# One mask of the first unit moved to ScalarE and GpSimd, and a new order of the early loads, in a fused gated-attention and feed-forward kernel

## The chip, the cores and the metric

The kernel runs on one core of one Trainium2 chip. The metric is the device time of one execution in microseconds (us); the median of three executions before the change is 182.77 us. The profiled execution of the kernel before spans 181.1 us from its first to its last instruction.

## What is computed

For 4 batches and 8 heads, a recurrence runs over 768 tokens with a state of 48x48 per head; the output, laid out as 3072 tokens by 384, goes through a two-layer feed-forward net with an exact gelu between. Cut to what matters:

```
f = 1 / (1 + exp(-f_logit))
for t in range(768):
    state = f[t][:, None] * state + outer(k[t], v[t])     # per batch and head, 48 x 48
    y[t]  = q[t] @ state
h   = x @ w_in                      # x: 3072 x 384 (all y), w_in: 384 x 2048
out = gelu_exact(h) @ w_out         # w_out: 2048 x 384
```

Inputs and the output are float32 in HBM.

## The kernel before, in words

**Tiling.** Tokens are cut into 24 chunks of 128; two chunks make a *unit* (12 of them, numbered u = 0 to 11). For a unit the recurrence is done in chunk form: decays from `f_logit` (Exp and Ln on ScalarE, cumulative sums on TensorE, then two more Exp), scaled q and k (`sc`, line 576), their transposes (`T`, line 611), scores inside the chunk (`A`, line 784), a triangular mask on them (`mask_scores`, line 621; normally one VectorE product per 128x512 tile, line 631, four for a unit), products with v (`YI`, line 826), the carried state (`S`, lines 806, 655, 657, 662; `YX`, line 705), and a transpose of the result (`XT`, line 691) that gives the feed-forward's input tile `xT`. Units 0 to 4 use a paired layout, in which a partition holds two neighbouring tokens; later units use a natural one.

**Feed-forward.** For each unit `ffn_group` makes 8 steps `F1` (line 875, six matmuls of 128x256 each, into one of four PSUM banks), one Gelu after each (line 885, ScalarE), and then `F2` (line 896), four steps of four matmuls for each of the two chunks, and stores of 128x384. `w_in` lies in three tiles: `win0` holds the columns 0 to 1023 (four of the eight F1 steps), `win1` 1024 to 1535 (two steps), `win2` 1536 to 2047 (two steps). `w_out` lies in four tiles `wout0` to `wout3`, one for each F2 step of a chunk. The profile and the lists of instructions count the tiles of one kernel through: there `win` 70, 71, 72 are `win0`, `win1`, `win2`, and `sc_99`, `sc_100` are the third unit's.

**Order of the work.** No engine's order is written out by hand. Each operation is given to a planner (`Plan`, line 85) with an engine, a duration, dependencies, buffers and a priority; `run` (line 116) places them one after another, by earliest start and then priority, and the instructions are issued in that order. Each engine then runs its list strictly in order. The priorities get a small random term, whose seeds are the list `SEEDS`, one for each unit. So a change of seeds reorders instructions on all engines without adding any.

**Loads.** The list `LOADS` gives the order of the transfers: `f2` is the logits of unit 2, `k2`, `q2`, `v2` its k, q and v, `i0` to `i2` the tiles `win0` to `win2`, `o0` to `o3` the tiles of `w_out`, `u4` all four inputs of unit 4 (`i3` names nothing and is passed over). Inputs of units are issued by SyncE and run on the DMA queue that the profile calls q1; weights are issued by GpSimd, which also casts them to bfloat16, and run on q0. The two queues are kept from overtaking one another by *gates* (`load`, line 382): where the queue changes from one entry to the next, the new transfer waits until an earlier one of the other queue has landed:

```
gate = None
if i and order[i - 1][0] != eng:
    back = 4 if eng == "pool" else 2
    for j in range(i - back, -1, -1):
        if order[j][0] != eng:
            gate = order[j][1]
            break
```

So a load on GpSimd looks four entries back and then on to the next one of SyncE's, and a load on SyncE two entries back. An entry whose predecessor is on its own queue gets no gate.

**Table sets.** Exp and Ln are in one table set of ScalarE and Gelu in another; at each change from one to the other a table load is issued (line 953).

**Junk matmuls.** In the first 30 us, where the plan leaves TensorE idle, matmuls on a tile `junk` are put in (line 947); they compute nothing.

Of the kernel before, what the change touches and what calls it, by code (L numbers as in the profile page):

```python
# [24 lines left out]

SPREAD, SEED = (1.0, 97)

SEEDS = [1643, 41, 3215, 1275, 2533, 2502, 823, 887, 1264, 763, 2447, 3095]

NUDGE = {}  # L30
XA = 0.0
# [53 lines left out]
class Plan:  # L85
# [30 lines left out]
    def run(self):  # L116
        free = dict.fromkeys(list(LAT), 0.7)
        free["DMA"] = 1.8
        rng = random.Random(SEED)
        own = [random.Random(x) for x in SEEDS]  # L120
        for o in self.ops:
            if o.prio > -5:
                k = min(max(int(o.prio % 1000) // 20, 0), len(SEEDS) - 1)
                o.prio += rng.uniform(-SPREAD, SPREAD)
                if SEEDS[k]:
                    w = (0.5, 1.0, 3.0, 8.0)[SEEDS[k] % 4]
                    o.prio += own[k].uniform(-w, w)
# [105 lines left out]
G1D = [2, 3, 4]  # L233
YJ = [2, 3, 4]
ROWS = [16, 17, 18, 19]
AMX = []
WARM = 30.0
LOADS = ['f0', 'k0', 'v0', 'q0', 'f1', 'v1', 'k1', 'q1', 'i0', 'k2', 'f2', 'v2', 'q2', 'i1', 'i2', 'i3', 'o0', 'o1', 'o3', 'o2', 'f3', 'k3', 'q3', 'u4', 'v3']
LOADS += [f"u{n}" for n in range(12) if f"u{n}" not in LOADS and f"c{2 * n}" not in LOADS and f"f{n}" not in LOADS]


@with_exitstack
def kernel(
# [185 lines left out]
    wo_src = moe_w_out.rearrange("(r p j) m -> r p j m", r=4, j=4)  # L429
    for what in LOADS:  # L430
        m = int(what[1:])
# [189 lines left out]
    def mask_scores(aps, ams, key, nm, rd, pr, mk, mkey):  # L621
        for hh in range(2):
            pl = key[1:] + (hh,) in GAM
            if key[1:] + (hh,) in AMX:
                P.add("ACT", 0.50, lambda hh=hh: nc.scalar.copy(ams[hh].t().rearrange("p h t -> p (h t)"), aps[hh].t()),
# [361 lines left out]
```

## Time and profile before

| what | value |
|---|---|
| median of 3 executions | 182.77 us (182.22 to 183.18) |
| span of the profiled execution | 181.1 us |
| TensorE busy | 171.7 us (95%), 10.4 us of it junk |
| ScalarE busy | 125.2 us (69%), 15 table loads of 1283 ns at line 953 |
| VectorE busy | 96.3 us (53%) |
| GpSimd busy | 53.6 us (30%) |
| first F1 matmul | 20.67 us |

TensorE is the engine with the most work. Its busy time must be read with care: junk is counted in it, and matmuls overlap, so that a busy TensorE need not be at its peak. The questions to ask of this profile are when TensorE begins work that counts, and what it waits for after that.

### The profile page before, as it was taken

To read this page: it belongs to the slowest core of one execution; us is meant where nothing else is said; L and a number is where in the kernel's file an instruction comes from. 1 tells how busy PE (TensorE), PEld (TensorE's weight loads), DVE (VectorE), ACT (ScalarE), POOL (GpSimd) and SP (SyncE) were. 2 spreads that over 40 slices of the span, in tenths; PEclk is the share of its full clock that TensorE was granted. 3 is DMA by queue.
4 is the path that set the end of the run, shared out by engine and by line. 5 is a ranking of instruction groups with operands and counts; after the bars stand their busy time and mean duration, and the time that the engine had idled before them with its cause. 6 is when DMAs were issued, how large, how long until landed. Compare 5 with 4: busy or idle time off the path is not lost.

```text
span 181.1 us, 4916 instructions
## 1 busy us (share of the span) xinstructions
PE 171.7 (95%) x1990; PEld 132.3 (73%) x1990; DVE 96.3 (53%) x194; ACT 125.2 (69%) x212; POOL 53.6 (30%) x116
## 2 busy tenths in 40 slices
PE   7788889999999999988999999999999999999993
PEld 2356669966787688785779689976697986886972
DVE  5289750058898564244896692527691625362110
ACT  2775198963899189999967759777585578560720
POOL 7657870003043641140176113112435110300000
PEclk9999999999999999999999999999999999999999
DMA  6999999949997898999999999999999872814102
GB/s 148 261 261 226 268 170 203 200 115 267 278 266 142 186 197 170 249 227 171 216 179 213 215 175 207 195 187 189 185 245 181 181 162 47 166 37 91 43 0 87
DMA packets 106998, 32.61 MB, mean 180 GB/s; under 512 B 102113, under 2 KB 106081, under 8 KB 106977
## 3 DMA queue, kind: packets, MB, share of 16 engines
q1 hardware_dynamic: 105056, 29.07, 79.7%
q0 software_dynamic: 1776, 3.15, 9.8%
q8 instruction: 15, 0.25, 0.6%
q10 hardware_dynamic: 144, 0.10, 0.2%
q14 instruction: 7, 0.05, 0.1%
HBM read 25.17 MB, written 4.72 MB: 165 GB/s over the span
## 4 chain that ended last, share of the span: by engine, by line
PE 64%; ACT 15%; DMA 15%; SPq 3%; issue 1%; DVE 0%; DVEq 0%
PE ps L875 26%; PE ps L896 25%; ACT gT L885 7%; DMA fl<-in_f_logit_dram 7%; DMA win<-in_moe_w_in_dram 5%; ACT L953 4%; SPq L449 3%; DMA kq<-sc 2%; PE ps L722 2%; PE ps L758 2%; PE ps L917 1%; ACT gt L549 1%; PE ps L521 1%; PE ps L699 1%; PE ps L745 1%
## 5 line engine op out<-in xcount | busy, mean ns | idle before, releaser
L885 ACT ACTIVATE gT<-ps 128x512 bf16<-128x512 f32 x96 | 57.5, 671 | 24.6 <-PE ps L875 23.0
L875 PE MATMUL ps<-xT,win 128*128 128x256 bf16 x576 | 68.7, 273 | 1.3 <-ACT gT L885 0.9
L896 PE MATMUL ps<-wout,gT 128*128 128x384 bf16 x368 | 66.0, 326 | 0.0
L875 PEld LDWEIGHTS <-win 128*128 128x128 bf16 x576 | 61.6, 114 | 3.9 <-issue 1.2
L896 PEld LDWEIGHTS <-gT 128*128 128x128 bf16 x368 | 34.2, 98 | 19.5
L583 POOL CAST vb<-vt 128x384 bf16<-128x384 f32 x22 | 12.6, 584 | 52.5 <-DMA vt<-in_v_dram 52.4
L631 DVE TENSOR_TENSOR am<-ps,mask 128x512 bf16<-128x512 f32 x28 | 17.6, 684 | 15.1 <-PE ps L722 15.1
L901 DVE COPY osb<-ps 128x384 f32<-128x384 f32 x20 | 11.1, 556 | 25.9 <-PE ps L896 18.2
L657 POOL TENSOR_TENSOR tn<-rr,gl 128x384 f32<-128x384 f32 x16 | 14.0, 872 | 35.2 <-DVE rr L655 34.6
L576 DVE TENSOR_TENSOR sc<-qt,gt 128x384 bf16<-128x384 f32 x23 | 14.0, 616 | 13.7 <-ACT gt L549 13.7
L576 DVE TENSOR_TENSOR sc<-kt,rg 128x384 bf16<-128x384 f32 x23 | 13.5, 597 | 11.3 <-ACT rg L543 11.3
L953 ACT ACT_TABLE_LOAD x15 | 19.2, 1283 | 0.3
L662 POOL CAST sb<-tn 48x192 bf16<-48x192 f32 x40 | 14.8, 371 | 11.6 <-DVE tn L651 6.6
L494 ACT ACTIVATE fl<-fl 128x768 f32<-128x768 f32 x12 | 10.1, 842 | 10.5 <-DMA fl<-in_f_logit_dram 10.5
L675 DVE CAST yb<-ps 128x384 bf16<-128x384 f32 x22 | 11.9, 555 | 7.4 <-PE ps L758 3.7
L631 DVE TENSOR_TENSOR am<-ps,maskp 128x512 bf16<-128x512 f32 x20 | 12.5, 684 | 2.2 <-PE ps L784 1.4
L543 ACT ACTIVATE rg<-ps 128x384 f32<-128x384 f32 x21 | 10.3, 503 | 4.4 <-PE ps L523 2.8
L549 ACT ACTIVATE gt<-ps 128x384 f32<-128x384 f32 x21 | 10.2, 503 | 3.9 <-PE ps L523 3.3
L947 PE MATMUL ps<-junk 128*128 128x512 bf16 (+3 forms) x36 | 10.4, 423 | 2.1 <-POOL junk L939 1.3
L655 DVE TENSOR_TENSOR rr<-ps,tn 128x384 f32<-128x384 f32 x16 | 8.9, 553 | 3.5 <-POOL tn L657 1.8
L497 ACT ACTIVATE lf<-fl 128x768 bf16<-128x768 f32 x12 | 10.1, 843 | 0.4
L947 PEld LDWEIGHTS <-junk 128*128 128x128 bf16 x36 | 3.6, 111 | 6.2 <-issue 3.5
(74 smaller groups left out, 130.4 us busy)
## 6 DMA issues: line engine op xcount, KB each, us to landing
out_dram<-osb SPq DMA_DIRECT2D x19, 192.0 KB, 3.1
fl<-in_f_logit_dram SPq DMA_DIRECT2D x14, 192.0 KB, 3.8
kt<-in_k_dram SPq DMA_DIRECT2D x14, 192.0 KB, 3.8
qt<-in_q_dram SPq DMA_DIRECT2D x14, 192.0 KB, 3.7
vt<-in_v_dram SPq DMA_DIRECT2D x14, 192.0 KB, 3.9
fl<-in_f_logit_dram SPq DMA_DIRECT2D x5, 384.0 KB, 6.2
kt<-in_k_dram SPq DMA_DIRECT2D x5, 384.0 KB, 6.2
vt<-in_v_dram SPq DMA_DIRECT2D x5, 384.0 KB, 5.7
```

Of the source, the lines that this page charges most:

```text
L549: P.add("ACT", 0.40, lambda g=gps[j], gtv=gtv: nc.scalar.activation(gtv(), g.t()[:, 0:HD].rearrange("q (p h d) -> q p h d", h=2, d=D), AF. ...
L576: P.add("POOL" if pl else "DVE", 0.80 if pl else 0.475, lambda a=a, y=y, j=j, w=w, pl=pl, b=(gtv if w else rg): (nc.gpsimd if pl else nc.v ...
L583: P.add("ACT" if hv else "POOL", 0.40 if hv else 0.47, lambda y=y, j=j, hv=hv: (nc.scalar.copy if hv else nc.gpsimd.tensor_copy)(y["vb"].t ...
L631: P.add("POOL" if pl else "DVE", 1.15 if pl else 0.61, lambda hh=hh, pl=pl: (nc.gpsimd if pl else nc.vector).tensor_tensor(ams[hh].t(), ap ...
L657: P.add("POOL", 0.83, lambda: nc.gpsimd.tensor_tensor(tn.t(), rr.t(), glb(), ALU.mult), rd=[("rr", n), ("gl", n)], wr=[("tn", n)], bufs=[r ...
L662: P.add("POOL", 0.36, lambda hh=hh: nc.gpsimd.tensor_copy(sb.t()[64 * hh:64 * hh + D, :, D * hh:D * hh + D], tn.t()[64 * hh:64 * hh + D, : ...
L675: P.add("ACT" if help_ else "DVE", 0.40 if help_ else 0.475, lambda: copier(help_)(yb.t()[:, i, :], yp.t()[:, 0:HD]), rd=[("yp", n)], wr=[ ...
L875: nc.tensor.matmul(hps.t()[:, i * tok:(i + 1) * tok].rearrange("a (s t) -> a s t", s=s), col(fo)[:, kk, :], xT.t()[:, :, kk, :], start=(kk ...
L885: nc.scalar.activation(to, fr, AF.Gelu)
L896: nc.tensor.matmul(op.t()[:, 0:d_model], gT.t()[:, fo, s_ * C:(s_ + 1) * C], wout[fo // 4][:, fo % 4, :], start=(fo == 0), stop=(fo == FO ...
L947: nc.tensor.matmul(o.opens.t()[:, 0:w], junk[:, 0:C], junk[:, 0:w], start=True, stop=True, skip_group_check=True)
L953: nc.scalar.preload_act_table_set({"exp": "natural_log_exp_and_others", "gelu": "gelu_and_others"}[o.table])
```

## The change

Three edits, and their consequences in the order of the instructions:

```diff
-SEEDS = [1643, 41, 3215, 1275, 2533, 2502, 823, 887, 1264, 763, 2447, 3095]
+SEEDS = [410, 2974, 3123, 787, 3638, 3000, 447, 988, 2575, 1888, 1815, 299]
...
-AMX = []
+AMX = [(0, 0, 1)]
...
-LOADS = ['f0', 'k0', 'v0', 'q0', 'f1', 'v1', 'k1', 'q1', 'i0', 'k2', 'f2', 'v2', 'q2', 'i1', 'i2', 'i3', 'o0', 'o1', 'o3', 'o2', 'f3', 'k3', 'q3', 'u4', 'v3']
+LOADS = ['f0', 'k0', 'v0', 'q0', 'f1', 'v1', 'k1', 'q1', 'f2', 'i2', 'i0', 'k2', 'v2', 'q2', 'i3', 'o0', 'o1', 'i1', 'o3', 'o2', 'f3', 'k3', 'q3', 'u4', 'v3']
```

`AMX` takes one of unit 0's four mask products off VectorE: ScalarE copies the scores from PSUM to SBUF (line 625), and GpSimd multiplies them there with the mask in place (line 627). `LOADS` brings the third unit's logits `f2` ahead of the weights, so that its decays can be computed before ScalarE goes over to Gelu, and brings `win2` ahead of `win0`, so that two of the eight F1 steps can start on a smaller tile; `win1` goes behind two tiles of `w_out`. `SEEDS` gives a new draw of the order.

In the compiled order of the instructions this reads as follows. The third unit's Exp, Ln and its other decay operations (lines 494 to 570) stand before the first table load for Gelu; before the change only its Exp and Ln did. The first F1 steps are two on `win2`, between the two halves of unit 1's score matmuls. The transposes of the third unit's scaled k and q (line 611) stand among the first unit's F1 steps; before, they stood behind all sixteen F1 steps of units 0 and 1. ScalarE has 21 table loads at line 953, before 15. The gates come out anew:

| transfer | waits for, before | waits for, after |
|---|---|---|
| `win0` (i0) | f1 landed | nothing (follows i2 on its queue) |
| `win2` (i2) | nothing (follows i1) | v1 landed |
| `k2` | nothing | `win2` landed |
| `f2` | nothing | nothing |
| `win1` (i1) | k2 landed | nothing (follows o1) |
| `wout0` (o0) | nothing (follows i2) | f2 landed |
| `f3` | `wout3` (o3) landed | `wout3` (o3) landed |

## The prediction

> **What bounds the kernel now.** I read the windows first, then the chain that ended last, then TensorE's timeline and the DMA queues.
>
> ```profile
> 25.00:30.00 5.00, 4.21 (x42) 3.54 (x40) 1.04 (x3) 4.25 (x7) 1.49 (x3) 1.00 1.14 182
> 30.00:35.00 5.00, 5.00 (x49) 5.00 (x47) 0.00 (x0) 5.00 (x10) 0.00 (x0) 1.00 1.08 212
> 35.00:40.00 5.00, 5.00 (x39) 3.29 (x38) 1.88 (x4) 4.33 (x9) 0.00 (x0) 1.00 0.44 94
> ```
>
> The columns are TensorE, weight loads, VectorE, ScalarE, GpSimd (busy us and instructions), clock, DMA share, GB/s. From 30 us TensorE is full; its waits after that are 0.4 us at 55, 0.5 us at 79 and 0.4 us at 84. So the time is the moment from which TensorE does nothing but real work, plus the work left, plus 3 us from the last matmul to the end of the store. A change can win only ahead of about 27 us; a stall that it makes later comes back whole. The chain says what the start waits for:
>
> ```profile
> 10.84 9.78 DMA win<-in_moe_w_in_dram
> 20.67 2.16 PE ps L875 x18
> ```
>
> `win0` is issued at 10.84 and lands at 20.6, and the first F1 follows at once. Then, on TensorE:
>
> ```profile
> 26.38 1.13 PE L947 MATMUL ps<-junk 128*128 128x512 bf16 x5 [0.79 <-ACT gT L885]
> 27.35 8.02 PE L875 MATMUL ps<-xT,win 128*128 128x256 bf16 x72
> 35.21 4.06 PE L896 MATMUL ps<-wout,gT 128*128 128x384 bf16 x24
> 39.11 0.61 PE L611 MATMUL ps<-ident,sc 128*128 128x128 bf16 x8
> ```
>
> From 25.4 to 27.4 TensorE waits for Gelu (2 us, more than half of it junk); then 12 F1 steps without a break, 24 matmuls of F2, and only at 39.1 the third unit's transposes. So k2 and q2 are not wanted before 38 us. The last view is the DMA queues, from 16 to 18 us and from 20 to 22 us:
>
> ```profile
> q0 software_dynamic: 168, 0.34, 90.9%
> q1 hardware_dynamic: 167, 0.06, 19.0%
> ```
> ```profile
> q1 hardware_dynamic: 1470, 0.55, 123.0%
> q0 software_dynamic: 2, 0.00, 0.6%
> ```
>
> (Packets, MB, share of 16 engines.) While `win0` is under way, both queues get the same number of packets. But one of q0 is 2 KB and one of q1 384 B, so q1 moves 0.06 MB in 2 us; alone it moves 0.55. The issues show it too: k2, issued just ahead of `win0`, takes 10.7 us to land, k1 6.2.
>
> ```profile
> kt<-in_k_dram SPq DMA_DIRECT2D x1, 384.0 KB, 10.7
> ```
>
> **What the Trainium skill says.** "DMA: Bandwidth & Descriptors", section "Queues, rings and completion order": each DMA engine goes round robin over its queues, packet by packet. The trace agrees (168 to 167). The same page, "Latency and other measured facts", has two of the 16 engines usually slower; no view here names an engine, but q0 still has 2 packets after 20 us, when an average engine should be done at 19.1 (below). "TensorE: Matmul & The Clock Gate", "What's actually happening": after about 3.4 us idle the array runs at half rate, until busy for about as long. The trace shows the cold start alone: the first 12 junk matmuls take 4.59 us (383 ns each), four later ones 0.92 us (230 each). "ScalarE: Activation LUTs", "What ACT_TABLE_LOAD costs", gives 1283 ns and a drain of 1380; the trace has the 1283, and only 0.3 us idle before all 15, so I take no drain.
>
> **The change, part by part.**
>
> *The mask.* VectorE loses one product of 684 ns. ScalarE gains a 128x512 copy from PSUM, between the 384-column copies (486 ns) and the Gelu of 512 (671): 0.6 us. GpSimd gains a product, not shown in this form: between its 384-column cast scaled by 512/384 (584 to 780 ns) and its 384-column float32 product scaled so (872 to 1163); I take 1.1. Behind the copy wait unit 1's decays, of which one v cast now comes later; behind the product unit 1's scaled k and q. YI of unit 0, at 15.09 before, moves by +0.2. Unit 1's scores move from 18.7 to about 19.5. Both lie ahead of the weights' landing: 0.
>
> *f2 early.* It takes k2's place at 10.32 on SyncE and follows q1 (landed 15.0). 1024 packets at 1376 in 2 us are 1.5 us: landed 16.5, for 22.5 before. ScalarE does unit 2's decays from about 18.6 to 23.2, loads the Gelu table until 24.5, and the 2 us wait at 25.4 goes.
>
> *win2, win0.* GpSimd issues `win2` behind a state product at about 12.4 (v1 lands at 5.87+6.2=12.1) and `win0` at once after. `win1`, of the same size, took 7.3 us from issue: `win2` lands at 19.7. `win0` follows on the queue: 24 packets an engine, with the pair time (one packet of each queue) 2x16/167=0.19 us, less 0.023 (32/1376) while q1 is empty: from 18.5 to 22.7 on an average engine, landing about 24.5. So the two F1 steps on `win2` run at about 20, those on `win0` from 24.8. Were that all: at 27.35 before, four F1 (2.6 us) and XT (0.5) were done; at 24.8 after, two F1 and no XT. Gain 27.35-24.8-1.3-0.5=0.75 us.
>
> *The new gates.* This is the step that decides. k2 waits on SyncE for `win2`'s landing, and v2 and q2 queue behind it: first packets at about 19.7+1.1=20.8 (the first load of all: issued 0.74, packets from about 1.9). `wout0`, gated by f2 alone, is issued at about 18.4, with `wout1` and `win1` right behind. So when k2 begins, q0 holds, for an average engine, 10 packets of `win0`, 8+8 of `wout` (128 of 3 KB each) and 24 of `win1` (1 KB): 50. k2 has 64 an engine and gets one for one. Times of one: `wout` 0.215+0.023 (149 packets in 32 to 34 us, 2x16/149), 1 KB 0.113+0.023 (24 to 26 us: 263 of q0 and 95 of q1 in 2x16). Sum 10x0.19+16x0.24+24x0.136=9.0, and 14x0.023=0.3: k2's last packet at 30.1, landed 31.1. `win0` began at about 14.5 (126 packets by 16 us, at 84 a us), so an average engine needed 4.6 us, the last one 5.6 (packets after 20 us): 1.2 times; over 9 us that is 1.8 more, 32.9. I take 32.5. q0 is then empty, so v2 lands at 34.0 and q2 at 35.5.
>
> Who waits: VectorE holds the third unit's scaled k (`sc_99`) in its strict list, TensorE its transposes behind only two F1 steps on `win0` and the XT. TensorE reaches them at 24.8+1.3+0.5=26.6 and stands until 32.5+0.65=33.2, although eight of the twelve F1 steps queued behind have their weights. After 6.6 us idle it starts cold: transposes 0.4, F1 1.3, transposes 0.4, F1 1.3: 36.6, warm by then; S (v2 at 34.0 plus two GpSimd casts, 35.3) 36.9; F1 37.5; transposes of q (35.5+0.6) 37.8; F1 38.4; VectorE's state sum and last scaled q after S, 38.0; transposes 38.6. From there it is full. Done then: 8 of the 16 F1, all 16 transposes, S. Before, at 38.6: 16 F1 and 3.4 us of F2, no transposes. Lag: 8x0.655+3.4-0.9-0.25=7.5 us. TensorE is saturated after that, so nothing gives it back: **182.8+7.5=190.3**.
>
> *wout3, wout2, f3.* `wout3` is issued behind the casts of v2 and a state product, at about 38.5, and lands about 43; f3, gated by it, about 47, for 41.9 before. ScalarE comes to it at about 48, F2 to `wout2` at about 48 too: 0, narrowly.
>
> *Seeds and table loads.* Six more loads are 6x1.283=7.7 us of ScalarE, which is 69% busy (73% then). They cost only where four PSUM banks of F1 are full and wait for Gelu: 0 to 4 us. I take 0, as F2 and attention stand between. The rest of the draw moves the same matmuls about: 0.
>
> **The rivals.**
>
> (A) Starved loads, as above: 190.3; with an average engine's k2 and no cold clock 188, with the slow engine's and a late f3 194. For it: the equal packet counts, the gates in the compiled order. Against: no window shows q1 beside 3 KB packets.
>
> (B) q1 gets its share, k2 lands by 25 and q2 by 28: nothing stalls, the gain of 0.75 us stays: **182.0**, some 1 us less if the new draw also takes away the later waits of 1.3 us, some 1 more if `win1` (behind 4 us of `wout`) is late. For it: the fast q1 of 20 to 22 us, if `wout` were issued late. Against: 168 to 167.
>
> (C) k2 is not the bound, but ScalarE with its 21 table loads is, in half of the six added: 182.0+3x1.28=**185.8**. For it: ScalarE 16.9 of 20 us from 80 to 100. Against: TensorE waited for Gelu 0.9 us in all after 27 us.
>
> **How the numbers follow.** A 0.74, B 0.14 (0.10 of it faster by over 0.5%, 0.04 within), C 0.12. Faster 0.10, same 0.04, slower 0.86. The likeliest is 190.3. The range takes in A with both ends of its costs and most of C, up to 195 where a late f3 and some table loads come on top; down to 184, below which lies B.
>
> **What would show it.** TensorE idle from about 26 to 33 us ahead of line 611, released by VectorE's `sc` at line 576, itself released by the DMA of `kt`; k2's time to landing over 11 us; equal packet counts of q0 and q1 from 21 to 30 us; unit 2's decays ahead of the first Gelu; first F1 on `win0` near 24.8. I am wrong if k2 lands before 27 us, or if TensorE meets line 611 without a wait.

## The result and the profile after

The changed kernel takes 188.19 us (median of 4 executions, 186.92 to 189.44) against 182.50 of the kernel before: a ratio of 1.030, 95% interval 1.023 to 1.038. It is slower by 5.5 us by this ratio (the two medians lie 5.7 us apart), where 7.5 were forecast. The profiled execution spans 185.2 us, 181.1 before.

The windows of the changed kernel, with the columns as before:

```profile
20.00:25.00 5.00, 5.00 (x61) 2.90 (x60) 3.30 (x7) 2.25 (x5) 2.19 (x5) 0.73 1.10 211
25.00:30.00 5.00, 4.03 (x72) 2.97 (x70) 2.22 (x4) 4.97 (x9) 0.89 (x3) 1.00 1.16 243
30.00:35.00 5.00, 3.80 (x44) 3.51 (x45) 3.32 (x8) 2.30 (x4) 1.54 (x3) 1.00 0.39 83
35.00:40.00 5.00, 5.00 (x74) 4.45 (x72) 3.51 (x6) 3.71 (x6) 2.13 (x5) 1.00 0.67 107
```

TensorE is full from 35 us on, not from 30 as before; and from 20 to 25 us, where its busy time looks full, it was granted 0.73 of its clock. The chain that ended last, in this stretch:

```profile
11.49 0.83 POOL tn L657
...
12.39 7.02 DMA win<-in_moe_w_in_dram
...
19.43 11.13 DMA kt<-in_k_dram
...
30.58 0.57 DVE sc L576
...
31.20 0.40 PE ps L611 x4
31.59 0.66 PE ps L875 x6
```

Before, the chain went from `win0` straight to F1. Now it goes from GpSimd's state product to `win2`, from its landing over the new gate to k2, from k2 to VectorE's scaled k, and from there to the transposes. TensorE's timeline shows the meeting:

```profile
27.19 0.85 PE L875 MATMUL ps<-xT,win 128*128 128x256 bf16 x6
27.88 0.33 PE L691 MATMUL ps<-ident,yb 128*128 128x128 bf16 x3
28.05 0.82 PE L875 MATMUL ps<-xT,win 128*128 128x256 bf16 x6
28.70 0.33 PE L691 MATMUL ps<-ident,yb 128*128 128x128 bf16 x3
31.20 0.40 PE L611 MATMUL ps<-ident,sc 128*128 128x128 bf16 x4 [2.17 <-DVE sc L576]
31.43 0.82 PE L875 MATMUL ps<-xT,win 128*128 128x256 bf16 x6
```

Two F1 steps on `win0` and the XT stand ahead of line 611; then come 2.17 us of nothing, although eight F1 steps queued behind have their weights. The list of TensorE's waits in this kernel:

```profile
PE ps L611 <- DVE sc L576: 3.8, 4, 2.2
```

(us in all, times, longest.) No wait for Gelu is in that list, with 21 table loads. The queues from 22 to 24 us and from 24 to 26 us:

```profile
q0 software_dynamic: 147, 0.40, 100.8%
q1 hardware_dynamic: 67, 0.03, 6.9%
```
```profile
q0 software_dynamic: 179, 0.33, 87.9%
q1 hardware_dynamic: 180, 0.07, 19.1%
```

k2 moves 0.03 MB and then 0.07 MB in 2 us each, beside `wout` and `win1`. In the first of the two windows its packets begin only at about 22.9 us; from 23 to 24 us there are 74 of q0 and 64 of q1. k2 takes 11.1 us to land, v2 12.1 and q2 12.7, counted from issue.

### The profile page after: what moved, and what is told of

Its sections match the earlier page's. It is cut to its first block, busy times and chain, and to the rows that moved or that the text cites. A ratio compares the mean times of both kernels' runs of the same rounds, so it can differ in the third digit from the quotient of the medians.

```text
span 185.2 us, 4914 instructions
## 1 busy us (share of the span) xinstructions
PE 174.2 (94%) x1989; PEld 132.5 (72%) x1989; DVE 97.4 (53%) x193; ACT 133.5 (72%) x219; POOL 54.1 (29%) x117
## 4 chain that ended last, share of the span: by engine, by line
PE 67%; DMA 15%; ACT 10%; DVE 4%; SPq 1%; issue 1%; POOL 1%; DVEq 0%; ACTq 0%
PE ps L875 27%; PE ps L896 27%; DMA kt<-in_k_dram 6%; ACT gT L885 5%; DMA win<-in_moe_w_in_dram 4%; DMA qt<-in_q_dram 3%; DMA kq<-sc 2%; PE ps L722 2%; DVE sc L576 2%; ACT L953 2%; PE ps L758 2%; PE ps L917 1%; SPq L449 1%; PE ps L521 1%; PE ps L699 1%
## 5 line engine op out<-in xcount | busy, mean ns | idle before, releaser
L875 PE MATMUL ps<-xT,win 128*128 128x256 bf16 x576 | 70.9, 274 | 0.0
L875 PEld LDWEIGHTS <-win 128*128 128x128 bf16 x576 | 60.9, 114 | 3.0 <-issue 0.5
L583 POOL CAST vb<-vt 128x384 bf16<-128x384 f32 x22 | 11.8, 547 | 61.4 <-DMA vt<-in_v_dram 61.3
L901 DVE COPY osb<-ps 128x384 f32<-128x384 f32 x20 | 11.1, 555 | 28.6 <-PE ps L896 28.2
L631 DVE TENSOR_TENSOR am<-ps,mask 128x512 bf16<-128x512 f32 x28 | 17.6, 682 | 13.2 <-PE ps L722 13.2
L662 POOL CAST sb<-tn 48x192 bf16<-48x192 f32 x40 | 15.1, 377 | 16.0 <-DVE tn L651 10.1
L576 DVE TENSOR_TENSOR sc<-qt,gt 128x384 bf16<-128x384 f32 x23 | 15.3, 681 | 1.6 <-DMA qt<-in_q_dram 1.5
L631 DVE TENSOR_TENSOR am<-ps,maskp 128x512 bf16<-128x512 f32 x19 | 11.9, 684 | 7.6 <-PE ps L784 7.6
L947 PE MATMUL ps<-junk 128*128 128x512 bf16 (+3 forms) x35 | 10.9, 454 | 1.3 <-POOL junk L939 1.3
L611 PE MATMUL ps<-ident,sc 128*128 128x128 bf16 x64 | 6.0, 226 | 4.3 <-DVE sc L576 3.8
```

What stands on the lines that cost most here:

```text
L576: P.add("POOL" if pl else "DVE", 0.80 if pl else 0.475, lambda a=a, y=y, j=j, w=w, pl=pl, b=(gtv if w else rg): (nc.gpsimd if pl else nc.v ...
L583: P.add("ACT" if hv else "POOL", 0.40 if hv else 0.47, lambda y=y, j=j, hv=hv: (nc.scalar.copy if hv else nc.gpsimd.tensor_copy)(y["vb"].t ...
L631: P.add("POOL" if pl else "DVE", 1.15 if pl else 0.61, lambda hh=hh, pl=pl: (nc.gpsimd if pl else nc.vector).tensor_tensor(ams[hh].t(), ap ...
L662: P.add("POOL", 0.36, lambda hh=hh: nc.gpsimd.tensor_copy(sb.t()[64 * hh:64 * hh + D, :, D * hh:D * hh + D], tn.t()[64 * hh:64 * hh + D, : ...
L875: nc.tensor.matmul(hps.t()[:, i * tok:(i + 1) * tok].rearrange("a (s t) -> a s t", s=s), col(fo)[:, kk, :], xT.t()[:, :, kk, :], start=(kk ...
L901: P.add("DVE" if od else "ACT", 0.475 if od else 0.40, lambda op=op, osb=osb, od=od: copier(not od)(osb.t(), op.t()[:, 0:d_model]), rd=[(" ...
```

## The experiments

The medians stand beside those of the kernel before on the same chip: 182.31 us for the first four runs, 182.74 for the next four, 182.08 for the three after them and 182.18 for the last. Except where it is said, each engine keeps its order of instructions, so that one thing changes at a time.

**1. The gate of k2 dropped.** Only k2's wait for `win2` goes:

```diff
-            if gate is not None:
+            if gate is not None and name not in ('kt2',):
```

> Theory (starved loads): every instruction stands as in the changed kernel, but k2 no longer waits for win2's landing, so k2, v2 and q2 go ahead behind f2, from about 15.5 us. k2 lands by about 20 us instead of 30.5. The wait of 2.2 us at the third unit's transposes (line 611) goes, with the smaller ones behind v2 and q2 (about 1 us): 185 us, 2.5 to 3.5 less than the changed kernel's 188.2. Rival (the mask product on GpSimd): the loss is made before 27 us by VectorE's 2.4 us product, the wait at line 611 only takes the place of another: 187.5 or more.

Measured: 187.56 us, ratio 1.026 (1.023 to 1.030). k2 is issued at 11.64, 8 us earlier, and lands only 1.3 us earlier. VectorE's timeline:

```profile
29.27 0.56 DVE L576 TENSOR_TENSOR sc<-kt,rg 128x384 bf16<-128x384 f32 x1 [1.36 <-DMA kt<-in_k_dram]
...
33.44 0.56 DVE L576 TENSOR_TENSOR sc<-qt,gt 128x384 bf16<-128x384 f32 x1 [2.62 <-DMA qt<-in_q_dram]
```

Its issue, in KB and us to landing:

```profile
kt<-in_k_dram SPq DMA_DIRECT2D x1, 384.0 KB, 17.6
```

So the gate is not what holds k2: without it the transfer takes 17.6 us instead of 11.1, and my 185 us, with k2 landed by 20 us, is missed. The wait stays on the loads, so this is no support for a cause elsewhere either, although that rival's number was hit.

**2. The mask back on VectorE.** ScalarE's copy and GpSimd's product give way to one VectorE product at the same place:

```diff
-nc.scalar.copy(ams[hh].t()..., aps[hh].t())
-nc.gpsimd.tensor_tensor(ams[hh].t(), ams[hh].t(), mk..., ALU.mult)
+nc.vector.tensor_tensor(ams[hh].t(), aps[hh].t()..., mk..., ALU.mult)
```

> The fourth mask product of unit 0 is on VectorE again; no other instruction moves in any engine's order. Theory (starved loads): k2's landing near 30.5 us still sets the restart, so TensorE comes earlier to the transposes of the third unit and waits longer there (over 3 us at line 611, 2.2 in the changed kernel): within 0.7 us of 188.2. Rival (the mask product on GpSimd): VectorE's product of unit 1's scaled q falls from 2.4 us to under 1, first F1 on win0 comes at 25 instead of 27.2 and the whole time falls by about 2 us, to 186.

Measured: 189.39 us, 1.037 (1.034 to 1.040). On TensorE:

```profile
25.49 0.84 PE L875 MATMUL ps<-xT,win 128*128 128x256 bf16 x6
...
31.41 0.61 PE L611 MATMUL ps<-ident,sc 128*128 128x128 bf16 x4 [4.09 <-DVE sc L576]
31.81 1.48 PE L875 MATMUL ps<-xT,win 128*128 128x256 bf16 x6
```

F1 on `win0` comes 1.7 us earlier and TensorE waits 1.9 us longer. After 4.09 us of idling an F1 step takes 1.48 us; after 2.17 us in the changed kernel it took 0.82. The median is 1.2 us above that of the changed kernel, outside the 0.7 us that I had allowed, though the intervals of the two ratios overlap. Coming earlier to a wait whose end is fixed gains nothing.

**3. Both edits together.**

> Both edits at once: k2 free and the mask on VectorE. If each takes away its own part of the loss, first F1 on win0 comes near 25 us, nothing waits at line 611 for loads, and the time is 182.5 to 183.5, the kernel before within 0.5%. If the new seeds with their six more table loads cost something of their own, 184 or more remains.

Measured: 188.00 us, 1.030 (1.026 to 1.035), k2 17.2 us to landing. The forecast missed, for the reason seen in run 1: freeing the gate doesn't free k2.

**4. The weights later.** The gate stays; GpSimd issues `wout0`, `wout1` and `win1` only behind the casts of v2 (`VC5` is the second of them):

```diff
     P.run()
+    moved = [o for o in P.placed if o.name in ("io0", "io1", "ii1")]
+    rest = [o for o in P.placed if o not in moved]
+    at = max(i for i, o in enumerate(rest) if o.name == "VC5") + 1
+    P.placed = rest[:at] + moved + rest[at:]
```

> The gate of k2 stays, but GpSimd issues wout0, wout1 and win1 behind the casts of v2, so only win0 stands beside k2 in the queues. Theory (starvation by packets, and not the gate alone): k2 lands at about 24.5 us, v2 and q2 by 28, the wait at line 611 falls below 0.5 us; win1 lands some 6 us later, at about 34, just ahead of its first use near 36: 185 to 186. Rival (the gate alone makes k2 late, whatever else is queued): k2 still takes about 11 us to land and the time stays at 188.

Measured: 184.69 us, 1.012 (1.007 to 1.016). k2, under the same gate:

```profile
kt<-in_k_dram SPq DMA_DIRECT2D x1, 384.0 KB, 5.3
```

It lands at 24.3 instead of 30.6, v2 takes 6.8 us and q2 7.4, and VectorE's scaled k waits for no load. Only the place of three issues on GpSimd has changed, and 3.4 us of the 5.5 are back (1.8% of 182). GpSimd's time is not what was freed, for after the three issues in the changed kernel it stood idle for 0.39 us. Under the same gate, and issued at nearly the same time (19.05, before 19.43), k2 takes half as long: this shows the starvation. What remains shows on TensorE:

```profile
22.61 1.47 PE L875 MATMUL ps<-xT,win 128*128 128x256 bf16 x6
...
28.28 0.84 PE L875 MATMUL ps<-xT,win 128*128 128x256 bf16 x6
```

The F1 on `win2` runs at the slow clock, and F1 on `win0` begins at 28.28, where my forecast had 24.8. This profiled execution, of 185.75 us, is the slowest of the six, which begin at 183.57.

**5. Run 4 with the mask on VectorE.**

> e4_late_wout with the fourth mask product of unit 0 back on VectorE, nothing else moved. In e4 nothing waits for k2 any more and 2.4 us (1.2%) over the kernel before remain, lost between 20 and 30 us. If the mask's move makes them (GpSimd's products meet VectorE's, which then takes 2.4 us), first F1 on win0 comes at about 26.5 us, not 28.3, and the time is about 183.0. If the seeds or the table loads make them, it stays at 184.5.

Measured: 185.19 us, 1.014 (1.010 to 1.018), the same as run 4 within the intervals. No cost and no gain of the mask can be seen, here as in run 2 against the changed kernel. F1 on `win0` begins at 25.64, not at 28.28, without a gain in the median; the profiled execution of run 5 is the fastest of its six (183.81 us) and that of run 4 the slowest, so that the two profiles can't be set against each other, and `win1` is already waited for here, for 0.42 us. VectorE's timeline gave the next clue, a product that took 0.55 us in other places:

```profile
14.95 2.38 DVE L576 TENSOR_TENSOR sc<-kt,rg 128x384 bf16<-128x384 f32 x1
```

**6 to 8. One part of the change alone.** In the kernel before, one line each of `LOADS`, `AMX` or `SEEDS` is replaced by that of the change, and the planner lays everything out anew.

> The kernel before with the new LOADS alone; the planner sets a new order with the old seeds (11 table loads). The third unit's transposes come early here too, behind two F1 steps on win0. Theory (starved loads): k2 takes over 11 us and lands near 30, TensorE waits 2 us or more at line 611: 185 to 187. Rival (the seeds or the mask make the loss): 182 to 183.

> The kernel before with the new AMX alone (27 table loads, as the planner places it with the old seeds). Theory: with the old loads TensorE waits for win0 until 20.6 us anyway, which hides the mask: 182.5 to 183.5. Rival (mask): GpSimd's products meet VectorE's here too, unit 1's scores come 2 us later: 184 to 185. If table loads are what costs, 12 more give up to 15 us more ScalarE work and the time goes over 186.

> The kernel before with the new SEEDS alone (21 table loads). Theory (the seeds are neutral): within 0.7% of the kernel before, 181.5 to 183.5, k2 landing near 21 us. Rival (the draw or its six more table loads cost): 184 or more, with waits for Gelu on TensorE in the second half.

Measured: 199.53 us (1.092), 194.69 (1.066) and 193.83 (1.061), intervals of 0.3 to 0.5% to either side. With the loads alone TensorE waits longest at the same place:

```profile
PE ps L611 <- DVE sc L576: 6.8, 3, 5.7
```

k2 takes 11.1 us to land, and VectorE stands 6.2 us for it ahead of its scaled k. That bears out the starvation once more. The rest can't be laid to the parts: all three lose 11 us or more against the kernel before, most of it between 60 and 170 us, far from the edits (TensorE is busy for 15.0 of the 20 us from 100 to 120 in the first, 16.7 from 120 to 140 in the second and 15.1 from 80 to 100 in the third, for 19.5 to 20 before), and the table loads come out at 11, 27 and 21. The numbers of two rivals were passed ("over 186" for the table loads, "184 or more" for the draw), but TensorE's waits for Gelu are only 3.9 us in all in run 7 and 3.2 in run 8. With the seeds alone TensorE's clock, in 40 slices, dips near 100 us:

```profile
PEclk9999999999999999999975999999999999999999
```

These runs suggest that a list of seeds fits only the plan for which it was drawn. They tell nothing of the mask or the seeds as such, and the forecasts for them missed.

**9. The early f2 alone, in the kernel before.** SyncE issues f2 ahead of k2; nothing else moves (`win1` gets f2's landing as its gate, to keep its time):

```diff
+    ik, jf = [[i for i, o in enumerate(P.placed) if o.name == n][0] for n in ("kt2", "fl2")]
+    P.placed[ik], P.placed[jf] = P.placed[jf], P.placed[ik]
...
-                    ins.ins, gate.inst.ins.name,
+                    ins.ins, (gate if name != 'i1' else [x for _, x in order if x.name == 'fl2'][0]).inst.ins.name,
```

> The kernel before with every engine's order kept, but SyncE issues f2 ahead of k2 (win1's gate moves from k2 to f2, so that it is issued as early as before). In the kernel before TensorE waits 2 us for Gelu at 25.4 us, because f2 lands at 22.5, unit 2's Exp and Ln end at 24.3 and only then the table load can begin. Theory (the early f2 was the sound part of the change, the early win2 with its gate and the early wout the harmful one): f2 lands 1.5 to 3 us earlier, the first Gelu follows by as much, the wait of 2 us shrinks to below 0.6: 180.8 to 181.4 us. Rival (f2 beside win0 is starved just as k2 was, and lands no earlier than 22): 182.5, no difference.

Measured: 181.37 us, 0.996 (0.994 to 0.997), faster than both kernels. ScalarE:

```profile
20.99 0.85 ACT L494 ACTIVATE fl<-fl 128x768 f32<-128x768 f32 x1 [2.35 <-DMA fl<-in_f_logit_dram]
21.87 0.84 ACT L497 ACTIVATE lf<-fl 128x768 bf16<-128x768 f32 x1
22.73 1.28 ACT L953 ACT_TABLE_LOAD   x1
24.03 2.53 ACT L885 ACTIVATE gT<-ps 128x512 bf16<-128x512 f32 x4
```

and TensorE, from where it is full:

```profile
26.34 8.02 PE L875 MATMUL ps<-xT,win 128*128 128x256 bf16 x72
```

The first Gelu comes 1.6 us earlier (25.59 before) and the long run of F1 1.0 us earlier (27.35 before); 0.7 us of it reach the end. Five junk matmuls still stand in TensorE's list ahead of that run (25.37 to 26.34); a version without them was not tried.

**10. Run 4 with VectorE's product ahead of its cast.** In the changed kernel VectorE's scaled q of chunk 2 (`QP2`) stands behind the cast of chunk 0's result (`YB0`), and meets GpSimd's two products for the same unit. VectorE and then GpSimd in the changed kernel:

```profile
14.89 0.82 DVE L576 TENSOR_TENSOR sc<-kt,rg 128x384 bf16<-128x384 f32 x1 [0.57 <-ACT rg L543]
15.75 0.56 DVE L675 CAST yb<-ps 128x384 bf16<-128x384 f32 x1
16.22 2.42 DVE L576 TENSOR_TENSOR sc<-qt,gt 128x384 bf16<-128x384 f32 x1
```
```profile
14.12 1.16 POOL L627 TENSOR_TENSOR am<-am,maskp 128x512 bf16<-128x512 bf16 x1
...
16.29 0.98 POOL L576 TENSOR_TENSOR sc<-kt,rg 128x384 bf16<-128x384 f32 x1
17.23 0.99 POOL L576 TENSOR_TENSOR sc<-qt,gt 128x384 bf16<-128x384 f32 x1
```

The edit, on top of run 4, moves the product one place ahead:

```diff
+    iy, iq = [[i for i, o in enumerate(P.placed) if o.name == n][0] for n in ("YB0", "QP2")]
+    P.placed[iy:iq + 1] = [P.placed[iq]] + P.placed[iy:iq]
```

> The changed kernel with wout0, wout1 and win1 issued behind the casts of v2 (184.7 by itself), and VectorE's product of unit 1's scaled q put ahead of its cast yb, so that it no longer meets GpSimd's two products. Theory (what is left over 182.5 comes from VectorE standing behind GpSimd's products: 2.4 us for one product, unit 1's scores 3 us later than before, and the sparse TensorE that cools down in that time): the product takes 0.6 to 0.9 us, unit 1's scores start near 20 instead of 22, TensorE's clock stays above 0.9 between 17.5 and 25 us, and the time is 182.4 to 183.2. Rival (the 2 us left are those of the order of the work, with the third unit's part ahead of F1, and of late weights): the product is short, but the time stays at 184.3 to 185.

Measured: 184.39 us, 1.012 (1.010 to 1.014): the number of the rival. The profile bears out half of it, the late weights. The product takes 0.69 us, the scores start at 19.77, the clock is 1.00 in every window from 15 to 30 us, F1 on `win0` starts at 24.84 and the third unit's line 611 has no wait; and then comes a new wait, of my own making:

```profile
36.31 1.50 PE L875 MATMUL ps<-xT,win 128*128 128x256 bf16 x12 [1.58 <-DMA win<-in_moe_w_in_dram]
```

`win1`, issued at 28.5 as the last of the three postponed weights, came too late for a TensorE that was now early. So the run left open whether the rest of the order costs anything.

**11. That swap alone, in the changed kernel.**

> The changed kernel with that one swap on VectorE alone (product of unit 1's scaled q ahead of the cast yb). Theory (k2's landing at 30.5 sets TensorE's restart): the first F1 on win0 comes 1.5 to 2.4 us earlier, the wait at line 611 grows by as much, and the time stays: 187.7 to 189.4. Rival (the late product is a loss of its own that adds to the starved loads): 185.8 to 186.5.

Measured: 188.69 us, 1.036 (1.033 to 1.039), no faster than the changed kernel. F1 on `win0` starts at 24.97, 2.2 us earlier, and the gain goes into the wait:

```profile
31.00 0.61 PE L611 MATMUL ps<-ident,sc 128*128 128x128 bf16 x4 [4.20 <-DVE sc L576]
```

As in run 2, k2's landing sets the restart, and the rival's 185.8 to 186.5 is missed.

**12. Run 10 with `win1` first, and sooner.** The order is `win1`, `wout0`, `wout1`, behind the last state cast of unit 1 (`SB3`); `win1` is issued 4.6 us earlier than in run 10, the other two 2.6 us:

```diff
-    moved = [o for o in P.placed if o.name in ("io0", "io1", "ii1")]
+    moved = [[o for o in P.placed if o.name == n][0] for n in ("ii1", "io0", "io1")]
...
-    at = max(i for i, o in enumerate(rest) if o.name == "VC5") + 1
+    at = max(i for i, o in enumerate(rest) if o.name == "SB3") + 1
```

> The kernel of the run before last (late weights, VectorE's product ahead of its cast; 184.4), with win1 issued ahead of wout0 and wout1, and the three behind unit 1's last state cast instead of behind the casts of v2, some 5 us earlier. There TensorE was ahead of the kernel before until 34.7 us and then stood 1.6 us for win1, which landed at 36.3; GpSimd's queue had been empty from 20 to 28.5 us. Theory (late weights of my own making ate the gain): no wait for win1, k2 still lands by 25 and q2 by 28, nothing waits at line 611 for more than 0.5 us, and the time is 182.4 to 183.0, that is, equal to before. Rival (the rest of the order costs it): no wait for win1, but 183.8 to 184.6.

Measured: 182.78 us, 1.004 (1.002 to 1.006). k2 and `win1`, issued from 18 to 26 us:

```profile
kt<-in_k_dram SPq DMA_DIRECT2D x1, 384.0 KB, 5.2
...
win<-in_moe_w_in_dram POOLq DMA_DIRECT2D x1, 384.0 KB, 5.5
```

and the longest entries of TensorE's waits, apart from the start of the junk:

```profile
PE ps L875 <- DMA xT<-yb: 0.7, 1, 0.7
PE ps L611 <- DVE sc L576: 0.7, 2, 0.4
```

The wait for `win1` is gone, the chain through k2 too, and with them all but 0.6 us of the 5.5. Mask, seeds, 21 table loads, the order of f2, `win2`, `win0` and every gate of the inputs are still those of the change. (`win1` ahead of `wout` is the order of the kernel before; how much of the gain over run 10 comes from that order and how much from the earlier issue was not separated.) What had cost the time was the place of three weight issues on GpSimd, and behind it one VectorE product in GpSimd's way. The latter shows only once the weights are out of the way: freed alone it brings nothing (run 11), freed beside late weights 1.5 us (run 4 to run 12, with the earlier `win1`).

## Why the prediction was right, and where its sizes were off

**The forecast** was slower, by starvation of k2 behind weights that its gate does not cover. That is what happened: the chain of waits goes through `win2`, k2, `sc` and line 611; equal packet counts (180 to 179) show in the window from 24 to 26 us. Run 4 removes the starvation and gets 3.4 us back. What the forecast had wrong within this is the weight of k2's own gate: "The new gates" was to be the step that decides, and the sum begins with k2's wait for `win2`. Run 1 takes that wait away, and k2 lands only 1.3 us earlier, and the median falls by only 0.6 us, which is not clear of the noise. The weights on the other queue decide, with the gate or without it.

**The mis-sized term is k2's landing**: 32.5 forecast, 30.55 measured. For an average DMA engine my sum had k2's packets from 20.8 to 30.1 us. Counted on q1 they run from about 22.9 us to about 28.7, where the 1024th falls (k2 has 1024 of them, 64 an engine). They begin 2.1 us late: 3.4 us after the issue, where I took 1.1. In run 4, without `wout` and `win1` on q0, they begin some 2 us after theirs; equal packet counts don't explain the difference, and its cause is open. By then less was left on q0: about 36 packets an engine (575 in all from 23 to 30 us) in place of 50. So it is in part luck that the sum's landing, 31.1, came close to the measured one. To it I had added a slowest engine's share and taken 32.5, which is 2.4 us behind the average engine's last packet; by this count it was 1.9. Of the 1.95 us, about 1.4 lie in the average engine's sum and 0.5 in the addition. v2 and q2, put at 34.0 and 35.5, came with it: VectorE takes up the scaled q at 33.24.

**The second is the cold restart**, which I had put at about 1.5 us (two F1 at 1.3 instead of 0.655, and 0.2 on the first transposes). In the profiled execution it did not come: after 2.17 us of idling F1 ran at 0.82 us; after 4.1 to 4.2 us in runs 2 and 11 it ran at 1.48. This agrees with the 3.4 us of the Trainium skill, "TensorE: Matmul & The Clock Gate", section "What's actually happening". Taken together, 7.5-1.95-1.5=4.05 us, and the spans of the two profiled executions differ by 185.2-181.1=4.1. The medians differ by 5.7: two of the four executions were near 187 us, the profiled one among them, and two at 189.2 and 189.4, of which there is no profile. The mean clock was 0.991 in the profiled execution and in the one of 189.2, 0.981 in the one of 189.4, so the clock does not explain both, and what they lost is open.

**TensorE's arrival was off too.** I had F1 on `win0` at 24.8 and the stall from 26.6 to 33.2, 6.6 us; it was 27.19, and 29.0 to 31.2, 2.2 us. The step that failed here is "The mask: 0" with "unit 1's scores at about 19.5": they came at 21.7, because VectorE's next product stood 2.42 us where I counted it as before (0.89). With the swap of run 11 the scores come at 19.89 and F1 at 24.97, so the forecast fits a kernel without that meeting. As runs 2 and 11 show, the arrival changes the length of the wait and hardly its end (31.41 and 31.00 us, 31.20 in the changed kernel). But it decides on the cold restart: with F1 on `win0` at 25.49 and 24.97 the wait was long enough for one. So it is likely that the cold restart of the forecast failed to come because TensorE came late.

**f2 early** was right in kind: no wait of TensorE for Gelu is left. Its decays began at 20.04 instead of 18.6, behind the copy of unit 1's transposes, which came late with them. Run 9 puts a size to the idea: 0.7 us. That this is close to the 0.75 of the forecast is chance, since those were reckoned at F1 on `win0` from all the new loads together.

**win2 and win0** landed at 19.4 (forecast 19.7) and about 23.1 (24.5).

**Table loads, f3, seeds at 0**: run 12 has the seeds and the table loads and is 0.6 us above the kernel before; in the changed kernel f3 was issued at 40.2 (37.8 before) and no wait of TensorE is listed for it. That bounds seeds and table loads together, if the gain that rival B counted (0.75 us) was there to be eaten, at about 1.4 us. Rival C, 185.8, falls; rival B, "if `wout` were issued late", 182.0, is run 12 with 182.8.

## What to carry to other kernels

A gate between two queues orders only the two transfers that it names. Before moving loads, list for each moment what the other queue holds ungated, in packets and in bytes per packet: small packets beside large ones can get an equal count of packets and still few of the bytes (here 180 to 179 packets and 0.07 to 0.33 MB). When TensorE stands before a load, the way out is to move the competitor, not the consumer; and each postponed weight needs a date of its own, or it becomes the next wait. Take one sound part of a bundle back into the old order by hand (run 9), since a replanned whole tells little of a part (runs 6 to 8).

## What the runs showed of the hardware

**A VectorE product and GpSimd's products hold each other up.** In four meetings VectorE's product of two SBUF operands ended 0.42 or 0.43 us after the end of a GpSimd product: 18.64 behind two products that ended at 18.22 and 15.71 behind the mask product (15.28) in the changed kernel, 17.33 behind 16.91 in run 5, and 17.09 behind 16.67 in the kernel before. The Trainium skill, "SBUF — State Buffer", section "SBUF: two separate sides", says that VectorE with two SBUF inputs and GpSimd hold a shared pair of ports as an exclusive lock, whichever starts first, for the whole instruction. The traces agree with the lock. Who gets it next came out both ways. In the changed kernel and in run 5 a waiting VectorE did not get in between two GpSimd products that followed each other: hence 2.4 us for a product that takes 0.55 alone. In the kernel before it did: its product at 15.26 took 0.56 us, and of GpSimd's two products around it (14.32 and 15.27) the second took 1.40 us, where others take 0.98 or 0.99. VectorE's cast from PSUM beside GpSimd's casts (0.56 us at 15.75) was not held.

**Sparse work can lower the clock without a long wait.** In the changed kernel TensorE's clock was 0.73 from 20 to 25 us (0.50 from 20 to 22.5), with no wait listed of over 1 us between 15 and 22 us; from 17.5 to 20 us it was busy for 1.53 of 2.5 us. In run 11, with the same list of instructions on TensorE and only VectorE's product moved, it was busy for 2.31 us there, and the clock stayed at 1.00 up to 27.5 us. No threshold follows: in run 2 TensorE was busy for 1.06 of the 2.5 us from 15 to 17.5, and the clock stayed at 1.00.
